# Query and value loads of a fused attention and feed-forward kernel move from ScalarE's DMA queue to SyncE's

## The chip, the cores and the metric

The kernel runs on one core of one Trainium2 chip. The metric is the device time of one execution in microseconds, the median of several timed runs. A further execution was taken with the hardware profiler; its rows are those shown here. An engine's own instructions run on the engine; the DMAs that it issues go through its sequencer, in the order of its queue, and the transfers themselves run beside all engines.

## The reference

Attention over 4 batches, 8 heads, 576 positions and 64 dimensions, in which each query keeps its 32 largest scores; then two feed-forward layers of 512 to 2048 to 512, the first with a rational function between its two products, the second with `h * cos(h)`:

```
scores = scale * np.matmul(q, k.transpose(0, 1, 3, 2))
kth = np.partition(scores, -top_k, axis=-1)[..., -top_k:-top_k + 1]
scores = np.where(scores >= kth, scores, -1000000000.0)
scores = scores - np.max(scores, axis=-1, keepdims=True)
attn = np.exp(scores)
attn = attn / (np.sum(attn, axis=-1, keepdims=True) + 1e-09)
x = np.matmul(attn, v)                       # then (batch * seq, 512)
h = x @ w_in                                 # first layer
P = a[0] + a[1] * h + a[2] * h**2 + a[3] * h**3
Q = 1.0 + np.abs(b[0]) * np.abs(h) + np.abs(b[1]) * h**2
x = (P / (Q + 1e-06)) @ w_out
h = x @ w_in2                                # second layer
out = (h * np.cos(h)) @ w_out2
```

## The kernel before

The 2304 tokens are 9 blocks (`k`) of 256. Attention goes by units: 72 of them, each one tile of 128 queries and one pair of heads, eight units to a block. Units 0 to 63 take their queries from one batch; in units 64 to 71 a tile holds the last 64 queries of two batches, so each such unit takes two sets of keys and two of values.

One unit goes through `qk` (TensorE makes scores in PSUM, ScalarE copies them out to `sS`), `topk` (VectorE finds the 32 largest of each row with eight-way maxima and replacements in `e`, ScalarE takes the exponential, VectorE masks and sums) and `av` (TensorE transposes `e`, ScalarE copies the transposes out as `pt...`, TensorE multiplies them with the values `v` in L383 and L388, ScalarE copies the result out to `xs`). `norm` divides by the sums. Scores are made one unit ahead: `qk(i + 1)` stands before `topk(i)`.

Products are taken in float32 split into a high and a low part. Queries are split by `split_q`: ScalarE writes `qh`, GpSimd subtracts and writes `ql` (both from `qr`). In the first units (`n < 2`) the raw queries and keys go into the product unsplit (L296). Keys are split once and stored in DRAM (`kdr`, from `kraw`); later units load the split keys from there with `load_k`.

The weights are split in the same way at the start (`conv`, 64 pieces, with tiles `raw` and `cb`, stored with SyncE's DMAs at L230 to L266), and their low parts are later streamed from DRAM: `stream` at L419, four buffers (`NST`), one buffer freed by TensorE's matmuls on it. The streams are `lo` (from `w1lo` and `w2lo`), `w1ol` and `w2o`; they feed the products at L442, L499 and L554. The feed-forward work of a block runs beside the attention of later blocks.

The loads that the change touches:

- `load_q` issues one load for two units, 256 KB into `qr`, of which there is one buffer (`QRB = 1`). So a load waits until the queries before it have been read: by GpSimd's `ql` where they are split, by TensorE where they are raw. `attention` calls it in the second fifth of every even unit (`p == LQ`), two units ahead.
- `load_v` issues one load for two units (two loads for each of the units 64 to 71), 320 KB into `v`, of which there are two buffers (`VB = 2`), freed by the value matmuls. `attention` calls it in the first fifth of a unit.
- `load_k` issues the loads of split keys on ScalarE's queue, 44 of them.

What sets the order: `attention` yields five pieces a unit, and the feed-forward steps have due times in pieces. The text of the program gives priorities. The order of each engine's queue is laid when the program is built, by a planner that plays the program through with its own estimates of durations (`TileContext(nc, schedule_with_timeline_sim=True)`): an instruction is placed when what it waits for is done in that play. On the chip each queue then keeps that order. `A`, `V` and `G` are ScalarE, VectorE and GpSimd behind a wrapper (`Windowed`) that, up to piece `PA = 90` on ScalarE, keeps an instruction behind those of `WA = 12` pieces earlier on that engine, DMA issues included; `SP` is SyncE without such a wrapper. All engine instructions issued through the wrapper carry its line, L78.

Of the kernel before, what the change touches and what calls it, by code (L numbers as in the profile page):

```python
# [87 lines left out]
def body(tc, out, qt, kt, vt, ident_d, w1_d, w1o_d, a_d, b_d, w2_d, w2o_d):  # L88
    nc = tc.nc
    V, A, G = Windowed(tc, nc.vector, WIN, PM), Windowed(tc, nc.scalar, WA, PA), Windowed(tc, nc.gpsimd, WG, PG)  # L90
    PE, SP = nc.tensor, nc.sync

    with ExitStack() as ctx:
# [57 lines left out]
        def load_q(i):  # L151
            k, pr = units[i][0] // 2, units[i][1]
            raw = att.tile([P, 2, BT], F32, tag="qr", bufs=QRB, name=f"qr{i}")
            A.dma_start(out=raw, in_=qt[k, pr])
            qpair[i // 2] = (raw,)

        def split_q(i):
# [21 lines left out]
        def load_v(i):  # L179
            n, pr = units[i]  # L180
            if i % 2 and not mixed[i]:
                ins[i][0][1] = vlast[0]
                return
            for j, (b, _) in enumerate(qts[n]):
                v = kv.tile([P, VW], F32, tag="v", bufs=VB, name=f"v{i}_{b}")
                A.dma_start(out=v, in_=vt[b, pr])
                ins[i][j][1] = vlast[0] = v

        load_q(0)
        load_k(0)  # L190
        ident = cst.tile([P, P], F32)
# [445 lines left out]
        def attention():  # L637
            load_k(1)
            load_v(0)
            qk(0)  # L640
            prev = None
            nrm, fresh, held = [], [], []
            for i in range(nu + 1):
                if LQ == 0 and i % 2 == 0 and i + 2 < nu:
                    load_q(i + 2)
# [8 lines left out]
                for p in range(5):  # L654
                    if p == 0 and prev is not None:
                        next(prev)
                    next(t, None)
                    if p == 0:
                        if prev is not None:
                            next(prev)  # L660
                        next(t, None)
                        if prev is not None:
                            av(i - 1)
                            if i % 4 == 0:
                                nrm.append(norm((i - 1) // 8, (i - 1) // 4 % 2))
                                next(nrm[-1])
                                fresh.append(nrm[-1])
                        if 0 < i < nu:
                            load_v(i)
                    if p == LQ > 0 and i % 2 == 0 and i + 2 < nu:  # L670
                        load_q(i + 2)
                    if p == SQ and i % 2 == 0 and 8 <= i + 2 < nu:
                        split_q(i + 2)
                    if fresh and p == 1:
                        next(fresh.pop())
                    if len(nrm) == 2 and (p == 1 or p == 4):
                        next(nrm[0 if p == 1 else 1], None)
                        if p == 4:
                            nrm = []
                    yield  # L680
# [56 lines left out]
```

## Time and profile before

| | us |
|---|---|
| timed runs | 1435.71, 1440.75, 1442.73 |
| median | 1440.75 |
| profiled execution | 1434.87 |
| its span, from the first to the last instruction | 1433.1 |

| engine | busy us | share of the span |
|---|---|---|
| TensorE, matmuls (PE) | 1248.5 | 87% |
| VectorE (DVE) | 1247.9 | 87% |
| ScalarE (ACT) | 1080.7 | 75% |
| GpSimd (POOL) | 632.7 | 44% |

The mean granted clock of TensorE was 0.934 of full speed. Two DMA queues carry the data: SyncE's 261.99 MB, ScalarE's 51.39 MB.

The shares are averages over stages with different limits, so the busy times by stage are read beside them. In the rows, `out<-in` names what an instruction writes and reads; SPq and ACTq are the queues of SyncE and ScalarE, and their lines are DMA issues, which do not count as busy time of the engine. `[2.92 <-ACT qh L78]` behind an instruction says that its engine sat idle 2.92 us before it, and what ended that. In a table of waits, `DVE u <- ACT u: 27.1, 8, 5.9` says that VectorE's work on `u` waited for ScalarE's `u` 27.1 us in all, 8 times, at most 5.9 us.

### The profile page before, as it was taken

To read this page: it belongs to the slowest core of one execution; us is meant where nothing else is said; L and a number is where in the kernel's file an instruction comes from. 1 tells how busy PE (TensorE), PEld (TensorE's weight loads), DVE (VectorE), ACT (ScalarE), POOL (GpSimd) and SP (SyncE) were. 2 spreads that over 40 slices of the span, in tenths; PEclk is the share of its full clock that TensorE was granted. 3 is DMA by queue.
4 is the path that set the end of the run, shared out by engine and by line. 5 is a ranking of instruction groups with operands and counts; after the bars stand their busy time and mean duration, and the time that the engine had idled before them with its cause. 6 is when DMAs were issued, how large, how long until landed. Compare 5 with 4: busy or idle time off the path is not lost.

```text
span 1433.1 us, 24823 instructions
## 1 busy us (share of the span) xinstructions
PE 1248.5 (87%) x8944; PEld 1106.0 (77%) x8944; DVE 1247.9 (87%) x2477; ACT 1080.7 (75%) x1873; POOL 632.7 (44%) x439
## 2 busy tenths in 40 slices
PE   5676777667996999899989988998999999999997
PEld 2344565556985888799878978897998899988986
DVE  6999878899999999999999999999999999645633
ACT  6787788766875887688878786887887788866743
POOL 3657455544543544455555454553545454420000
PEclk9776798779999999999999999999999999999999
DMA  7986867773555656466675665565565777656686
GB/s 242 313 274 206 264 209 223 267 273 126 176 189 188 214 201 217 151 203 236 224 234 203 209 216 168 189 218 178 195 222 198 264 259 277 219 202 221 222 278 220
DMA packets 141547, 314.96 MB, mean 220 GB/s; under 512 B 12016, under 2 KB 28528, under 8 KB 141424
## 3 DMA queue, kind: packets, MB, share of 16 engines
q1 hardware_dynamic: 122832, 261.99, 54.4%
q10 hardware_dynamic: 18592, 51.39, 10.6%
q8 instruction: 70, 1.15, 0.3%
q14 instruction: 53, 0.43, 0.1%
HBM read 278.20 MB, written 35.13 MB: 219 GB/s over the span
## 4 chain that ended last, share of the span: by engine, by line
DVE 41%; PE 31%; ACT 11%; DMA 9%; issue 5%; POOL 2%; ACTq 0%; SPq 0%; DVEq 0%; POOLq 0%
DVE e L78 18%; DVE hd L78 10%; DVE u L78 6%; PE o L554 6%; PE h L440 4%; PE h L441 4%; PE h L442 4%; DVE cb L78 2%; DMA raw<-w 2%; DMA w2o<-w2o 2%; PE y L499 2%; PE y L497 2%; PE y L498 2%; ACT L78 2%; DVE q L78 2%
## 5 line engine op out<-in xcount | busy, mean ns | idle before, releaser
L78 DVE MAX8 hd<-e 128x8 f32<-128x288 f32 (+1 forms) x576 | 322.2, 594 | 0.0
L554 PE MATMUL o<-w2o,gg 128*128 128x512 f32 x864 | 228.7, 402 | 10.4 <-DMA w2o<-w2o 10.3
L78 DVE MATCH_REPLACE8 e<-hd,e 128x288 f32<-128x288 f32 (+1 forms) x432 | 230.6, 538 | 0.0
L554 PEld LDWEIGHTS o<-w2o,gg 128*128 128x128 f32 x864 | 155.7, 192 | 41.8 <-DMA w2o<-w2o 14.1
L78 DVE TENSOR_TENSOR e<-sS 128x576 f32<-128x576 f32 x144 | 164.4, 1178 | 26.9 <-ACT sS L78 13.6
L440 PE MATMUL h<-xh,w1hi 128*128 128x256 f32 x576 | 172.3, 299 | 13.4 <-ACT hs L78 6.4
L497 PE MATMUL y<-gg,w1o 128*128 128x256 f32 x576 | 168.0, 292 | 16.9 <-ACT gg L78 16.9
L440 PE MATMUL h<-x2h,w2hi 128*128 128x256 f32 x576 | 165.8, 288 | 12.3 <-ACT w L78 8.0
L498 PE MATMUL y<-gg,w1o 128*128 128x256 f32 x576 | 167.9, 292 | 6.6 <-POOL gg L78 6.5
L441 PE MATMUL h<-xl,w1hi 128*128 128x256 f32 x576 | 167.9, 292 | 2.3 <-DVE xl L78 2.3
L499 PE MATMUL y<-gg,w1ol 128*128 128x256 f32 x576 | 166.3, 289 | 3.5 <-DMA w1ol<-w1ol 3.4
L78 POOL TENSOR_TENSOR gg<-u,gg 128x512 fp32r<-128x512 f32 x64 | 94.4, 1474 | 169.4 <-ACT gg L78 145.9
L441 PE MATMUL h<-x2l,w2hi 128*128 128x256 f32 x576 | 165.0, 287 | 3.6 <-DVE x2l L78 3.6
L442 PE MATMUL h<-xh,lo 128*128 128x256 f32 x576 | 166.9, 290 | 0.0
L442 PE MATMUL h<-x2h,lo 128*128 128x256 f32 x576 | 164.7, 286 | 0.0
L78 POOL TENSOR_TENSOR u<-u,w 128x512 f32<-128x512 f32 x64 | 94.2, 1471 | 156.6 <-ACT u L78 156.4
L78 DVE SCALAR_TENSOR_TENSOR e<-sS,hd,e 128x576 f32<-128x576 f32 x144 | 140.8, 987 | 10.0 <-ACT e L78 9.7
L78 ACT ACTIVATE e<-sS,nb 128x576 f32<-128x576 f32 x144 | 109.1, 772 | 40.4 <-DVE hd L78 40.3
L78 POOL TENSOR_TENSOR cb<-cb,raw 128x512 int32<-128x512 int32 x64 | 93.7, 1466 | 97.9 <-DVE cb L78 80.5
L497 PEld LDWEIGHTS y<-gg,w1o 128*128 128x128 f32 x576 | 112.6, 195 | 22.3 <-ACT gg L78 20.2
L440 PEld LDWEIGHTS h<-xh,w1hi 128*128 128x128 f32 x576 | 114.0, 198 | 18.6 <-ACT hs L78 8.5
L78 POOL TENSOR_TENSOR rr<-rr,hs 128x512 f32<-128x512 f32 x56 | 79.3, 1436 | 104.0 <-ACT rr L78 103.9
(1166 smaller groups left out, 3720.1 us busy)
## 6 DMA issues: line engine op xcount, KB each, us to landing
w2o<-w2o SPq DMA_DIRECT2D x144, 512.0 KB, 4.2
lo<-w1lo SPq DMA_DIRECT2D x72, 512.0 KB, 4.1
w1ol<-w1ol SPq DMA_DIRECT2D x72, 512.0 KB, 4.1
lo<-w2lo SPq DMA_DIRECT2D x72, 512.0 KB, 4.4
k<-kdr ACTq DMA_DIRECT2D x44, 576.0 KB, 5.1
raw<-w SPq DMA_DIRECT2D x32, 512.0 KB, 5.2
v<-vt ACTq DMA_DIRECT2D x48, 320.0 KB, 4.4
qr<-qt ACTq DMA_DIRECT2D x36, 256.0 KB, 4.2
```

The lines of the kernel that those rows point to most:

```text
L78: r = f(*a, **k)
L440: PE.matmul(h[:, i, :], wh, xh[:, c, :], start=(c == 0), stop=False)
L441: PE.matmul(h[:, i, :], wh, xl[:, c, :], start=False, stop=False)
L442: PE.matmul(h[:, i, :], lo[:, i, c, :], xh[:, c, :], start=False, stop=(c == NCC - 1))
L497: PE.matmul(y[:, c, :], w1o[:, f, cs], gh[:, i, :], start=(f == 0 and c % 2 == 0), stop=False, skip_group_check=True)
L498: PE.matmul(y[:, c, :], w1o[:, f, cs], gl[:, i, :], start=False, stop=False, skip_group_check=True)
L499: PE.matmul(y[:, c, :], wl[:, i, cs], gh[:, i, :], start=False, stop=(f == NF - 1), skip_group_check=True)
L554: PE.matmul(o[:, t, :], l[:, i, ts], wt[i][:, r], start=(f == 0 and r == 0 and l is gh), stop=(f == NF - 1 and l is gl), skip_group_check= ...
```

## The change

The loads of queries and of values are issued by SyncE instead of ScalarE. Tiles, buffers, bytes and the places of the calls stay as they are.

```diff
         def load_q(i):
             k, pr = units[i][0] // 2, units[i][1]
             raw = att.tile([P, 2, BT], F32, tag="qr", bufs=QRB, name=f"qr{i}")
-            A.dma_start(out=raw, in_=qt[k, pr])
+            SP.dma_start(out=raw, in_=qt[k, pr])
             qpair[i // 2] = (raw,)
...
             for j, (b, _) in enumerate(qts[n]):
                 v = kv.tile([P, VW], F32, tag="v", bufs=VB, name=f"v{i}_{b}")
-                A.dma_start(out=v, in_=vt[b, pr])
+                SP.dma_start(out=v, in_=vt[b, pr])
                 ins[i][j][1] = vlast[0] = v
```

## Rows read from the trace of the kernel before

**Rows 1.** The page: busy us, share of the span and instructions of each engine.

```profile
PE 1248.5 (87%) x8944; PEld 1106.0 (77%) x8944; DVE 1247.9 (87%) x2477; ACT 1080.7 (75%) x1873; POOL 632.7 (44%) x439
```

**Rows 2.** Busy us by stage: stretch, length, engines, TensorE's clock, DMA share, GB/s.

```profile
0.00:360.00 360.00, 250.17 (x1287) 183.97 (x1288) 317.65 (x636) 267.62 (x501) 185.30 (x134) 0.80 0.73 240
360.00:1240.00 880.00, 820.07 (x6416) 759.53 (x6415) 842.92 (x1706) 698.85 (x1208) 431.10 (x293) 0.97 0.62 210
1240.00:1433.10 193.10, 178.31 (x1247) 162.48 (x1246) 87.36 (x136) 114.24 (x165) 16.28 (x13) 1.00 0.68 227
```

**Rows 3.** The page's chain that ended last, shares by engine.

```profile
DVE 41%; PE 31%; ACT 11%; DMA 9%; issue 5%; POOL 2%; ACTq 0%; SPq 0%; DVEq 0%; POOLq 0%
```

**Rows 4.** VectorE's waits: who waited for whom, us in total, times, longest.

```profile
DVE u L78 <- ACT u L78: 27.1, 8, 5.9
DVE cb L78 <- ACT cb L78: 20.9, 11, 3.9
```

**Rows 5.** Query and value issues: ns least, median, most; first and last start.

```profile
L78 ACTq DMA_DIRECT2D qr<-qt x36: 334/335/445, 0.7 to 1154.0; - x36
...
L78 ACTq DMA_DIRECT2D v<-vt x48: 334/335/550, 1.2 to 1240.7; - x48
```

**Rows 6.** ScalarE in order of time at a value load: start, length, instruction.

```profile
524.79 0.20 ACT L78 ACTIVATE nb<-hd 128x2 f32<-128x2 f32 x1 [1.32 <-DVE hd L78]
524.80 0.33 ACTq L78 DMA_DIRECT2D v<-vt  x1
524.90 0.62 ACT L78 ACTIVATE r<-w 128x512 f32<-128x512 f32 x1
```

**Rows 7.** GpSimd's subtraction, the load behind it, tile ql and its waiters.

```profile
717.38 1.73 POOL L78 TENSOR_TENSOR ql<-qr,qh 128x512 fp32r<-128x512 f32 x1 [2.92 <-ACT qh L78]
...
719.14 0.34 ACTq L78 DMA_DIRECT2D qr<-qt  x1
...
L78 POOL TENSOR_TENSOR ql<-qr,qh x32: 1268/1440/2185, 120.0 to 1187.9; 128x512 fp32r<-128x512 f32 x32
...
  ACT q L78: 0.6, 1
  ACT r L78: 0.6, 1
```

**Rows 8.** SyncE's largest waits: from 0 to 360, then from 360 to 1240.

```profile
SPq L230 <- POOL cb L78: 62.4, 42, 3.7
...
SPq L419 <- PE h L442: 381.1, 92, 11.5
```

**Rows 9.** SyncE's queue in order of time around 719 us.

```profile
718.41 0.32 SPq L419 DMA_DIRECT2D w2o<-w2o  x1
721.63 0.37 SPq L419 DMA_DIRECT2D lo<-w1lo  x1
```

**Rows 10.** Loads and first readers, by time (L383: first to last start).

```profile
110.33 0.35 ACTq L78 DMA_DIRECT2D qr<-qt  x1
...
115.47 0.62 ACT L78 ACTIVATE qh<-qr 128x512 fp32r<-128x512 f32 x1
...
488.39 0.34 ACTq L78 DMA_DIRECT2D v<-vt  x1
...
L383 PE MATMUL sx<-pt28t,v x2: 272/273/274, 541.6 to 541.7; 128*128 128x128 f32 x2
...
747.16 0.61 ACT L78 ACTIVATE qh<-qr 128x512 fp32r<-128x512 f32 x1
```

**Rows 11.** Tile w2o: its readers' idle time that its loads ended, times.

```profile
  DMA w2o<-w2o: 24.4, 23
```

**Rows 12.** Value matmuls of units 44, 52 and 60, as in rows 10.

```profile
L383 PE MATMUL sx<-pt44t,v x2: 273/274/274, 807.1 to 807.2; 128*128 128x128 f32 x2
...
L383 PE MATMUL sx<-pt52t,v x2: 272/274/275, 947.0 to 947.1; 128*128 128x128 f32 x2
...
L383 PE MATMUL sx<-pt60t,v x2: 272/273/274, 1078.7 to 1078.8; 128*128 128x128 f32 x2
```

## The prediction

> **What bounds the kernel now.** I read the page first, then a table of busy time by stage, then the chain, then the waits. On the page no engine is the bound by its average: TensorE and VectorE are busy 87% of the span each, ScalarE 75%, GpSimd 44% [rows 1]. So the table by stage comes next [rows 2]. In the first 360 us, where weights are split while attention already runs, VectorE is busy 317.65 us and TensorE runs at 0.80 of its clock. From 360 to 1240 us, where attention and both feed-forward passes overlap, VectorE is busy 842.92 of 880 us (96%) and TensorE 820.07 (93%). In the last 193 us attention is over, and TensorE has 178.31 us. VectorE sets the pace until 1240 us, TensorE after that. The chain agrees: VectorE 41%, TensorE 31%, ScalarE 11%, DMA 9% [rows 3]. ScalarE counts only where the others wait for it; VectorE's two largest such waits are 27.1 and 20.9 us [rows 4].
>
> **The change part by part.** It takes 84 DMA issues from ScalarE's queue, 36 of queries and 48 of values, and puts them into SyncE's [rows 5].
>
> *What ScalarE gets back.* One issue takes 0.335 us at the median, so 84 x 0.335 = 28.1 us of its queue. Does its arithmetic stand still meanwhile? At 524.80 us a value load is issued, 0.01 us after `nb` began; `nb` takes 0.20 us, and the next instruction starts at 524.90, before `nb` has ended [rows 6]. The issue lies beside the arithmetic and costs nothing there. What is left is a queue that waits. A query load waits until GpSimd has read the old queries: the subtraction `ql` begins at 717.38, takes 1.73 us and so ends at 719.11, and the load goes out at 719.14 [rows 7]. What ScalarE loses by this stands among those who waited for `ql`: `q` 0.6 us and `r` 0.6 us [rows 7]. The visible gain is 1.2 us of idle ScalarE, by its share of the chain 1.2 x 0.11 = 0.1 us. The upper bound takes all of the queue time at that share, 28.1 x 0.11 = 3.1 us. I take 0.1, since the rows show the overlap itself.
>
> *What SyncE gets.* The same 28.1 us, in a queue that mostly waits: in the 880 us of the middle its stream loads (L419) wait 381.1 us for TensorE in one group alone [rows 8]. There is room, and what counts is order. Stream loads are released by TensorE's matmuls, value loads by its value matmuls, and one engine in order releases both, so neither holds the other for long. A query load is released by GpSimd, so it can hold SyncE's queue; behind it stand loads of weights, and behind those TensorE. In the sample, SyncE's neighbours went out at 718.41 and 721.63, and the query load at 719.14 falls between them [rows 7, 9]: at that place the price is nothing. Laid one place earlier, it would push the load of 718.41 to about 719.45, 1.0 us late.
>
> The Trainium skill ("DMA: Bandwidth & Descriptors", "Anatomy of one DMA") says that DMA engines do not wait on semaphores; the issuing sequencer does, ahead of dispatch. The trace agrees: the query load went out 0.03 us after `ql` ended [rows 7]. By that rule a query load holds whatever stands behind it in SyncE's queue, and the sum would be the first rival's.
>
> *What hides a late load.* The values issued at 488.39 are first read at 541.6, 53 us later; the queries issued at 719.14 are split at 747.16, 28 us later [rows 7, 10]. Some microseconds more in SyncE's queue don't show there. Cover is thin in the first stage: queries issued at 110.33 are split at 115.47, 5.1 us from issue [rows 10]. I take zero, and keep that stage as a rival.
>
> *What stays.* Bytes, arithmetic and buffers are the same, and the loads of split keys stay on ScalarE.
>
> *Sum.* Minus 0.1 us, with bounds of minus 3.1 and, from the first rival, plus 57, on a profiled execution of 1434.87 us, of which 1433.1 are span: about 1435. The median of the three timed runs is 1440.75, 5.9 us higher; they spread from 1435.71 to 1442.73. The comparison is with the median, so the forecast is 1441 us, no change that can be measured. About 0.5% (7 us) is what a measurement of this kernel can tell from no change.
>
> **The rivals.**
>
> *Slower: the query load holds the weight stream.* Place: SyncE's queue, 360 to 1240 us. It decides where the load is laid ahead of a stream load whose buffer is free before `ql` has ended. Price at most: one `ql` (1.44 us at the median) and one issue (0.33) for each of the 32 splits [rows 7], 32 x 1.77 = 57 us. For it: readers of `w2o` sat idle 23 times for a load already (weight loads and matmuls counted apart), 24.4 us in all [rows 11], so that stream has loads without slack; and GpSimd sat idle 2.92 us for ScalarE before `ql` began [rows 7], so its end can come late. Against it: most loads of that stream have slack, and the sample has room on both sides. I take a quarter of the 57 us, 14: 1455 us. Chance 0.15.
>
> *Faster: ScalarE answers sooner.* VectorE's two largest waits for ScalarE are 48 us together [rows 4]. With 84 entries fewer ahead of what VectorE waits for, a quarter of that might close: 12 us, 1429 us. For it: ScalarE is on the chain with 11% [rows 3]. Against it: the overlap [rows 6]. Chance 0.12.
>
> *Either way: the queues are laid anew.* A queue's order is not that of the program text. The planner lays it when the program is built, by due order and its own estimates of durations; with 84 entries in another queue it may lay others differently, on every engine. What an order is worth can be read from repeated work: eight units of attention with one block of feed-forward. Their first value matmuls start at 541.6 (unit 28), 807.1 (unit 44), 947.0 (unit 52) and 1078.7 (unit 60) [rows 10, 12]. That is 265.5 us for two blocks, then 139.9, then 131.7: a mean of 134.3 us with a spread (standard deviation) of 3.8. Nine blocks laid anew and independently give 3.8 x 3 = 11 us around no change. Chance 0.35, of which 0.095 falls below minus 7 us, 0.16 within and 0.095 above plus 7.
>
> *Slower: early queries come late.* In the first 360 us SyncE's largest wait is for GpSimd, 62.4 us in 42 pieces of up to 3.7 us [rows 8]; a query load behind such pieces eats up the 5.1 us from issue to use. If five loads come 2 us late each, it is 10 us: 1451 us. Against it: scores are made one unit ahead of VectorE's use, so a late query needn't stop it. Chance 0.05.
>
> That the change does nothing would need the loads to stay where they are; they go to another queue, so I give that no chance.
>
> **How the numbers follow.** No change by the sum has 0.33. Within 0.5%: 0.33 + 0.16 = 0.49, say 0.48. Faster: 0.12 + 0.095 = 0.215, say 0.22. Slower: 0.15 + 0.05 + 0.095 = 0.295, say 0.30. The likeliest case is no change: 1441 us, with 1434 to 1448 as its own range. The whole range is 1425 to 1461. Its low end takes in the faster case and one spread and a half of newly laid queues (16 us below), its high end the slower cases at their taken price and almost two spreads (20 us above). What lies beyond is the slower case near its bound of 57 us and the tails, about one tenth.
>
> **What the profile after would show.** If I am right: 84 issues under SyncE with the same 0.33 us and none of these under ScalarE; busy VectorE and TensorE from 360 to 1240 us within a few microseconds of before; idle time for `w2o` still near 24 us. First rival: SyncE's waits for `ql` reach tens of microseconds, and TensorE's waits for stream loads grow by ten or more. Second: VectorE's waits for ScalarE shrink by ten or more. Third: the blocks' lengths change while nobody waits for a moved load, and unrelated instructions stand in another order. Fourth: waits for `qr` or `v` in the first 360 us. The forecast is wrong if the time moves by over 7 us; by which of these, the waits tell.

## The result and the profile after

The changed kernel is slower: the ratio to the kernel before is 1.0134, with an interval of 1.0102 to 1.0166; the medians of four executions each are 1456.34 us after and 1441.74 us before, 14.6 us apart (1.0101; the recorded ratio is not formed from these two medians, and it is the ratios that are compared below). The forecast was no change (1441 us). The time lies inside the range given, the direction was missed.

One caution for reading the rows: the profiled execution of the changed kernel took 1466.88 us (span 1465.1), the longest of its four (the others 1458.57, 1454.12 and 1453.96), while the one of before (1434.87) lay below its median. So the rows below show 32 us where the medians show 14.6; what they tell is where the time went, more than how much.

The page after, busy time of the engines and the chain that ended last, to be held against [rows 1] and [rows 3]:

```profile
span 1465.1 us, 24836 instructions
PE 1263.3 (86%) x8944; PEld 1111.6 (76%) x8944; DVE 1257.4 (86%) x2477; ACT 1078.0 (74%) x1873; POOL 623.3 (43%) x439
DVE 38%; PE 31%; DMA 13%; ACT 11%; issue 5%; POOL 2%; SPq 1%; ACTq 0%; DVEq 0%; POOLq 0%
```

Each engine runs as many instructions as before. ScalarE, the engine that was relieved, is as busy as it was (1078.0 against 1080.7 us) and holds the same 11% of the chain. VectorE is 9.5 us busier, with the same 2477 instructions.

Busy time by stage after, columns as in [rows 2]; attention now ends near 1275 us instead of 1240:

```profile
0.00:360.00 360.00, 253.28 (x1318) 184.32 (x1319) 317.78 (x634) 267.77 (x503) 183.15 (x135) 0.81 0.74 241
360.00:1275.00 915.00, 833.50 (x6414) 766.85 (x6414) 852.19 (x1708) 696.93 (x1209) 424.36 (x293) 0.96 0.61 202
1275.00:1465.00 190.00, 176.57 (x1217) 160.40 (x1215) 87.39 (x136) 113.27 (x163) 15.77 (x12) 0.99 0.70 229
```

The first and the last stage are what they were. The middle one does the same work (1708 instructions of VectorE against 1706) in 915 us instead of 880. The granted clock of TensorE there, 0.96, is close to the 0.97 of before; a kernel that follows below (the old queue in the new order) is as late with 0.97, so the clock isn't where the time went. The first value matmuls of units 28, 44, 52 and 60 tell the same (behind the durations stand the first and the last start, as in [rows 10] and [rows 12]):

```profile
L383 PE MATMUL sx<-pt28t,v x2: 273/274/275, 556.0 to 556.2; 128*128 128x128 f32 x2
...
L383 PE MATMUL sx<-pt44t,v x2: 271/273/275, 828.3 to 828.4; 128*128 128x128 f32 x2
...
L383 PE MATMUL sx<-pt52t,v x2: 273/274/274, 965.9 to 966.0; 128*128 128x128 f32 x2
...
L383 PE MATMUL sx<-pt60t,v x2: 272/274/275, 1104.8 to 1104.9; 128*128 128x128 f32 x2
```

Against before that is 14.4, 21.2, 18.9 and 26.1 us late: no single stall, but a loss that grows, and once shrinks, over the whole middle.

The moved loads, and what SyncE's queue waits for after (columns as in [rows 5] and [rows 8], the waits over the whole span):

```profile
L154 SPq DMA_DIRECT2D qr<-qt x36: 328/346/541, 0.7 to 1183.8; - x36
...
L186 SPq DMA_DIRECT2D v<-vt x48: 327/346/975, 3.1 to 1273.2; - x48
...
SPq L419 <- PE h L442: 405.4, 120, 11.0
...
SPq L186 <- PE sx L388: 53.9, 33, 5.0
...
SPq L154 <- POOL ql L78: 49.5, 25, 5.2
```

The change does what it says: 84 issues under SyncE, 0.346 us each. SyncE's queue now waits 49.5 us for `ql` and 53.9 us for the value matmuls. But behind those waits hardly anyone waits longer than before. The readers of the streams `lo` and `w1ol` sat idle for their loads 12.0 us instead of 8.7, and 13.2 in the kernel below that has the moved loads back on ScalarE. The readers of `w2o` did so no longer than before (24.4 us in [rows 11]):

```profile
  DMA w2o<-w2o: 22.3, 24
```

So where is the time? VectorE sets the pace until attention ends, so its account is the one to draw up. Before, it was busy 1160.57 of 1240 us and idle 79.4; after, 1169.97 of 1275 and idle 105.0. The 35 us are 9.4 of longer work and 25.6 of idling. Some 3 us of these 35 come of where the stages are cut: VectorE's last work before 1240 us ended at 1239.3, the same instruction after ended at 1271.3, 32 us later, which is the difference of the spans. The idling by what ended it, over the whole span, first some groups of before, then those of after (columns as in [rows 4]; the wait for ScalarE's `u`, 27.1 us before, lies behind the end of attention in both and isn't part of this account):

```profile
DVE e L78 <- ACT sS L78: 13.6, 6, 6.6
DVE e L78 <- ACT e L78: 9.7, 14, 2.2
DVE u L78 <- POOL u L78: 8.1, 8, 2.5
```

```profile
DVE u L78 <- ACT u L78: 26.1, 8, 5.0
DVE e L78 <- ACT e L78: 25.6, 19, 3.8
DVE cb L78 <- ACT cb L78: 23.2, 8, 4.3
...
DVE e L78 <- ACT sS L78: 15.9, 9, 5.3
DVE u L78 <- POOL u L78: 13.6, 10, 2.6
...
DVE e L78 <- PE pp20t L377: 6.3, 1, 6.3
```

The largest term is the wait for ScalarE's exponential, 9.7 to 25.6 us; then GpSimd's `u` with 5.5 more, `cb` and `sS` with 2.3 each (smaller groups shrank). The single wait for a transpose of 6.3 us (`pp20t`) stands out, but all waits for transposes together grew by only 1.5 (13.4 to 14.9). None of these is a load of queries or values, and none is an engine that got more to do. The instructions stand in another order. The two built programs, listed by the names of their instructions without those that only wait, differ in 3912 lines on TensorE (each program has 8160 matmuls there; an instruction that moved counts as two lines), in 1424 on ScalarE and 202 on SyncE (84 of each are the moved loads), and in 824 on VectorE.

The longest of those waits for the exponential can be followed back. Three engines in order of time, after:

```profile
1157.03 0.58 PE L299 MATMUL sx<-k,qh 128*128 128x288 f32 x1 [4.20 <-DMA k<-kdr]
...
1159.09 2.76 PE L554 MATMUL o<-w2o,gg 128*128 128x512 f32 x6
1161.64 0.89 PE L370 MATMUL pp64a<-ident,e 128*128 128x128 f32 x4
```

```profile
1162.57 0.60 ACT L78 ACTIVATE pt64a<-pp64a 128x512 f32<-128x512 f32 x1 [2.60 <-PE pp64a L370]
...
1163.75 0.65 ACT L78 ACTIVATE sS<-sx 128x576 f32<-128x576 f32 x1 [0.58 <-PE sx L301]
...
1164.30 1.44 ACT L78 ACTIVATE e<-sS,nb 128x576 f32<-128x576 f32 x2
```

```profile
1159.85 1.41 DVE L78 MAX8 hd<-e 128x8 f32<-128x576 f32 x2
1165.10 0.82 DVE L78 SCALAR_TENSOR_TENSOR e<-sS,hd,e 128x576 f32<-128x576 f32 x1 [3.85 <-ACT e L78]
```

VectorE's maxima, the last that it does to `e` ahead of the exponential, ended at 1161.26. But on ScalarE the exponential stands behind the copy `pt64a`, which waits for TensorE, and on TensorE the transposes stand behind six feed-forward matmuls and those behind scores that waited 4.20 us for split keys. Each queue keeps its order, so a delay on TensorE reaches VectorE through work that has nothing to do with it.

This wait shows how a delay travels along the queues, but it is not a price of the order itself. In the kernel below that has the same order on all engines, and the loads on ScalarE, the same instruction waited 0.19 us:

```profile
1158.10 0.82 DVE L78 SCALAR_TENSOR_TENSOR e<-sS,hd,e 128x576 f32<-128x576 f32 x1 [0.19 <-ACT e L78]
```

What began it after, a load of split keys issued at 1146.77 that TensorE still waited for at 1157, is one of 44, and the slowest of them took 9.6 us to land (at most 7.7 in the kernel before). A moved query load (1149.86) and a moved value load (1150.62) went out while it was under way; whether they slowed it is not shown.

### The profile page after: what moved, and what is told of

It is laid out like the page before. It is cut to its first block, busy times and chain, and to the rows that moved or that the text cites. A ratio compares the mean times of both kernels' runs of the same rounds, so it can differ in the third digit from the quotient of the medians.

```text
span 1465.1 us, 24836 instructions
## 1 busy us (share of the span) xinstructions
PE 1263.3 (86%) x8944; PEld 1111.6 (76%) x8944; DVE 1257.4 (86%) x2477; ACT 1078.0 (74%) x1873; POOL 623.3 (43%) x439
## 4 chain that ended last, share of the span: by engine, by line
DVE 38%; PE 31%; DMA 13%; ACT 11%; issue 5%; POOL 2%; SPq 1%; ACTq 0%; DVEq 0%; POOLq 0%
DVE e L78 17%; DVE hd L78 9%; PE o L554 7%; DVE u L78 6%; PE h L440 4%; PE h L441 4%; PE h L442 4%; DMA w2o<-w2o 2%; DVE cb L78 2%; PE y L499 2%; PE y L497 2%; DMA raw<-w 2%; PE y L498 2%; DMA kdr<-kraw 2%; DVE q L78 2%
## 5 line engine op out<-in xcount | busy, mean ns | idle before, releaser
L554 PE MATMUL o<-w2o,gg 128*128 128x512 f32 x864 | 235.5, 408 | 9.6 <-DMA w2o<-w2o 9.4
L78 DVE TENSOR_TENSOR e<-sS 128x576 f32<-128x576 f32 x144 | 173.5, 1241 | 31.1 <-ACT sS L78 15.9
L78 POOL TENSOR_TENSOR gg<-u,gg 128x512 fp32r<-128x512 f32 x64 | 92.2, 1440 | 185.4 <-ACT gg L78 174.0
L78 POOL TENSOR_TENSOR u<-u,w 128x512 f32<-128x512 f32 x64 | 88.8, 1388 | 179.9 <-ACT u L78 156.0
L78 DVE SCALAR_TENSOR_TENSOR e<-sS,hd,e 128x576 f32<-128x576 f32 x144 | 141.6, 991 | 26.1 <-ACT e L78 25.6
L440 PEld LDWEIGHTS h<-x2h,w2hi 128*128 128x128 f32 x576 | 111.7, 194 | 16.5 <-ACT w L78 12.2
L497 PEld LDWEIGHTS y<-gg,w1o 128*128 128x128 f32 x576 | 114.1, 198 | 12.7 <-ACT gg L78 10.3
```

The costliest lines, as they stand in the source:

```text
L78: r = f(*a, **k)
L440: PE.matmul(h[:, i, :], wh, xh[:, c, :], start=(c == 0), stop=False)
L497: PE.matmul(y[:, c, :], w1o[:, f, cs], gh[:, i, :], start=(f == 0 and c % 2 == 0), stop=False, skip_group_check=True)
L554: PE.matmul(o[:, t, :], l[:, i, ts], wt[i][:, r], start=(f == 0 and r == 0 and l is gh), stop=(f == NF - 1 and l is gl), skip_group_check= ...
```

## The experiments

Two theories were to be told apart. One: SyncE's queue is at fault, where loads that wait for `ql` hold the stream (the prediction's first rival). Two: the new order of all queues is at fault, whatever queue the loads are in (its third rival). What tells them apart is a program whose order is given instead of planned: `ORDER` lists the instructions of a program as it was built before, and each engine's are chained in that sequence, without a wait between them (the code is shown in part). A moved load stands at the place that the planner gave it in time.

```python
    for q in queues.values():
        q.sort(key=lambda x: place[x.name])
        for x, y in zip(q, q[1:]):
            tc.add_manual_dep(y, x.name, mybir.DependencyInfo(mybir.DependencyClass.NoSync, mybir.DependencyReason.DATA), reason="pin")
```

**The new queue in the old order.** The changed kernel, all engines in the order of before:

```diff
+ORDER = (
...
         body(tc, out, *aps)
+        pin(tc)
```

> The loads stand in SyncE's queue as in the changed kernel, but every engine keeps the order that it has in the kernel before (each queue chained by edges without a wait; the moved loads stand in SyncE's queue at the place that the planner gave them in time). Theory 'order' (the 14.6 us come from queues laid anew on other engines): within 5 us of before, about 1441 us. Theory 'hold' (a query load that waits for GpSimd's ql holds SyncE's weight stream): the loss stays, about 1455 us, with waits of SyncE for ql of some 50 us as in the changed kernel and more idle time of TensorE for stream loads.

Measured: 1439.16 us against 1440.0, ratio 1.0002 (0.9985 to 1.002). The loss is gone, with all 84 loads on SyncE; on TensorE and VectorE no instruction stands elsewhere than in the kernel before. SyncE's waits for `ql`, and the idling of the `w2o` readers, in this kernel:

```profile
SPq L154 <- POOL ql L78: 59.8, 25, 5.4
```

```profile
  DMA w2o<-w2o: 33.7, 36
```

Both are larger here than in the changed kernel (49.5 and 22.3). So neither is what made that one slow.

**The old queue in the new order.** The changed kernel's order on all engines, with the loads back on ScalarE (issued past the wrapper, which the change took them out of too):

```diff
-            SP.dma_start(out=raw, in_=qt[k, pr])
+            nc.scalar.dma_start(out=raw, in_=qt[k, pr])
...
-                SP.dma_start(out=v, in_=vt[b, pr])
+                nc.scalar.dma_start(out=v, in_=vt[b, pr])
...
+        pin(tc)
```

> The loads stand in ScalarE's queue as before, but every engine keeps the order that it has in the changed kernel. Theory 'order': the loss comes with the order, about 1456 us (1450 to 1462). Theory 'hold': SyncE's queue is free of the loads, so about 1441 us.

Measured: 1460.42 us, ratio 1.0155 (1.0127 to 1.0183). The loss is back without one load moved. Its profiled execution (1460.25) lies at its median, so its rows are the fairer ones for the order's price. From 360 to 1240 us VectorE gets through 1655 instructions where before it was 1706, at the granted clock of before (0.97):

```profile
360.00:1240.00 880.00, 796.37 (x6144) 731.87 (x6143) 826.88 (x1655) 674.48 (x1169) 409.82 (x283) 0.97 0.61 202
```

Two of VectorE's waits in it:

```profile
DVE e L78 <- ACT e L78: 20.4, 18, 2.7
...
DVE e L78 <- PE pp20t L377: 6.1, 1, 6.1
```

Next to each other, in us, from the rows of these four and of two kernels that follow further down:

| | before | new queue, old order | after | old queue, new order | TensorE's order kept | third order |
|---|---|---|---|---|---|---|
| VectorE busy | 1247.9 | 1248.2 | 1257.4 | 1258.2 | 1236.2 | 1249.8 |
| VectorE waits for the exponential | 9.7 | 11.3 | 25.6 | 20.4 | 16.7 | 18.6 |
| ScalarE waits for raw keys (`kraw`) | 4.3 | 10.2 | 17.6 | 17.8 | 5.8 | 7.5 |
| `w2o` readers idle for its loads | 24.4 | 33.7 | 22.3 | 24.7 | 28.6 | 17.7 |
| ratio | 1 | 1.0002 | 1.0134 | 1.0155 | 0.9995 | 0.9929 |

In the first four kernels the first two lines go by the order and not by the queue. The third goes by it in the main, but doubles with the queue alone (4.3 to 10.2). No line by itself ranks the kernels: the third order, the fastest, has 18.6 us of waits for the exponential, and the kernel with two small loads moved, further down, is slower than before with 8.8.

**One of the two loads alone**, in the planner's own order. Only the line of `load_q`, then only that of `load_v`:

```diff
-            A.dma_start(out=raw, in_=qt[k, pr])
+            SP.dma_start(out=raw, in_=qt[k, pr])
```

> Only the 36 query loads move to SyncE; values stay on ScalarE; queues laid anew by the planner. Theory 'hold': query loads alone wait for ql, so nearly all of the loss, 1452 to 1457 us. Theory 'order': a third order, its time not tied to the loads, anywhere from 1430 to 1460 us.

```diff
-                A.dma_start(out=v, in_=vt[b, pr])
+                SP.dma_start(out=v, in_=vt[b, pr])
```

> Only the 48 value loads move to SyncE; queries stay on ScalarE; queues laid anew by the planner. Theory 'hold': value loads are released by TensorE in order and hold nothing, so 1438 to 1445 us. Theory 'order': a fourth order, anywhere from 1430 to 1460 us.

Measured: 1431.28 us, ratio 0.9941 (0.992 to 0.9962) with the queries alone, and 1443.71 us, 1.0032 (1.001 to 1.0055) with the values alone. The queries are the loads that wait for `ql` (67.4 us in that kernel), and by the first theory they had to cost; that kernel is faster than before. The parts don't add up to the whole either: minus 0.6% and plus 0.3% against plus 1.3%.

**Both loads moved, in a third order**: the changed kernel, all engines in the order that the planner had laid with the queries alone on SyncE.

```diff
+ORDER = (
...
+        pin(tc)
```

> Both loads stand in SyncE's queue as in the changed kernel, but every engine keeps the order of e3_queries_only (where only the queries had moved), the fastest order so far at 1431 us. Theory 'order' (the queue costs nothing, the order everything): 1431 us, 1427 to 1436, and so faster than both kernels with the very queues of the changed one. If the values in SyncE's queue cost something in some orders: above 1436 us.

Measured: 1428.51 us against 1437.59, ratio 0.9929 (0.9902 to 0.9957). The very change that lost 1.3% gains 0.7% in another order. This version is faster than both kernels. Against the queries alone (0.9941), in the same order, it has the values on SyncE as well, and no loss by it.

**What the first rival costs where it acts.** The new queue in the old order, but 26 query loads, from the eleventh on, laid earlier in SyncE's queue: one place, then further. The expectations below speak of three places for the second kernel; in the queue that it ran with, each of the 26 stands two places earlier. Shown is the queue's order, not the list itself:

```diff
-    [stream load A] [stream load B] [stream load C] [query load]
+    [stream load A] [stream load B] [query load] [stream load C]
...
-    [stream load A] [stream load B] [stream load C] [query load]
+    [stream load A] [query load] [stream load B] [stream load C]
```

> As e6_early_query_loads, with the 26 query loads one place earlier instead of three. It looks for the point from which a held SyncE queue costs time. A hold costs only beyond the slack of the weight loads (TensorE's idle time for them was 33.7 us with no place moved and 124.6 with three): SyncE's waits for ql near 100 us, TensorE's idle time for w2o 40 to 70 us, 1441 to 1456 us. If the price grew evenly with places, 1440 + 46 / 3 = 1455 us.

> As e1_new_queue_old_order, but each of the 26 query loads from the eleventh on is laid three places earlier in SyncE's queue, so ahead of three weight loads or stores that it stood behind. This makes the hold that my prediction feared on purpose. Theory 'a hold costs where it is laid early': SyncE stands some 5 us longer at each, 26 times, weight loads have a few us of slack, so 1450 to 1540 us, with TensorE's idle time for stream loads up from some 30 us to over 100. Theory 'a held SyncE queue is harmless wherever': 1440 us.

Measured: one place 1448.31 us, ratio 1.0058 (1.0035 to 1.0081); two places 1485.92 us, 1.0326 (1.0297 to 1.0354). SyncE's waits for `ql` and TensorE's for `w2o`, first with no, then one, then two places:

```profile
SPq L154 <- POOL ql L78: 59.8, 25, 5.4
PE o L554 <- DMA w2o<-w2o: 14.0, 16, 2.0
```

```profile
SPq L154 <- POOL ql L78: 114.9, 27, 8.7
PE o L554 <- DMA w2o<-w2o: 27.2, 22, 3.5
```

```profile
SPq L154 <- POOL ql L78: 191.0, 27, 14.4
PE o L554 <- DMA w2o<-w2o: 57.9, 27, 7.8
```

Here the mechanism shows both its signs. TensorE's waits grow by 13.2 and by 43.9 us, and the ratios, of some 1438 us, make 8 and 47 us. Per load that is 0.3 us for one place and 1.8 for two.

**Moves that should do nothing.** Two small loads of coefficients at the start go from SyncE to ScalarE, in the kernel before:

```diff
-        SP.dma_start(out=coef[:, 0:4], in_=a_d)
-        SP.dma_start(out=coef[:, 4:6], in_=b_d)
+        nc.scalar.dma_start(out=coef[:, 0:4], in_=a_d)
+        nc.scalar.dma_start(out=coef[:, 4:6], in_=b_d)
```

> The kernel before, with queries and values on ScalarE as they were; only the two loads of constants at the start (2 KB and 1 KB, used once) are issued by ScalarE instead of SyncE. The work of the queues is the same, but the planner lays all queues anew. Theory 'order': the time moves by an amount that has nothing to do with the two loads, anywhere from 1430 to 1460 us. If orders don't matter as such and the loss is due to where queries and values stand: 1437 to 1444 us.

And the loads of queries and values stay on ScalarE but go past the wrapper that ties them to the pieces:

```diff
-            A.dma_start(out=raw, in_=qt[k, pr])
+            nc.scalar.dma_start(out=raw, in_=qt[k, pr])
...
-                A.dma_start(out=v, in_=vt[b, pr])
+                nc.scalar.dma_start(out=v, in_=vt[b, pr])
```

> The kernel before; queries and values stay on ScalarE's queue, but are issued without the wrapper that keeps ScalarE's instructions within 12 pieces of each other at the start (the change takes the loads out of that wrapper too). Theory 'order': again all queues are laid anew, anywhere from 1430 to 1460 us. If leaving the wrapper is what costs: about 1456 us.

Measured: 1448.53 us, ratio 1.0065 (1.0044 to 1.0086), and 1447.48 us, 1.0076 (1.0047 to 1.0105). TensorE's order differs from before in 3440 and 3078 lines. Two loads of a few numbers per partition, used from 6.38 us on in the kernel before, cost 0.65%. Not by coming late themselves: VectorE's wait for them was 6.4 us before, and with them on ScalarE it is

```profile
DVE nega L78 <- DMA coef<-ma: 5.1, 1, 5.1
```

That it is the order that the planner then lays follows from the runs with a given order; for these two kernels it was not tested by itself.

**Which engine's order it is.** The changed kernel with one engine alone in the order of before, the others laid anew by the planner:

```diff
+ORDER = (
...
+        pin(tc)
```

> The changed kernel, with only TensorE's queue kept in the order of the kernel before; the planner lays the other queues around it. If what was lost came in with the order of TensorE's queue (VectorE waiting for transposes and ScalarE's copies behind it): 1436 to 1446 us. If it came with the orders of ScalarE's or VectorE's queues: 1450 us or more.

> The changed kernel, with only ScalarE's compute instructions kept in the order of the kernel before. If the loss came in with ScalarE's order: 1436 to 1446 us. If with TensorE's or VectorE's: 1450 us or more. Since the planner lays every queue around the kept one, both this and the one before may come out near 1441 us; then no single queue holds the loss.

> The changed kernel, with only VectorE's queue kept in the order of the kernel before. TensorE's and ScalarE's queues still differ much from before. If VectorE's order holds the loss: 1436 to 1446 us. If TensorE's or ScalarE's does: 1450 us or more.

Measured: with TensorE's order kept 1438.86 us, 0.9995 (0.9972 to 1.0018); with ScalarE's 1449.69 us, 1.0064 (1.0045 to 1.0084); with VectorE's 1457.32 us, 1.0124 (1.0095 to 1.0152). VectorE sets the pace, yet keeping its order gives nothing back that can be measured, and keeping TensorE's gives all. One reservation: an order that is kept on one engine draws the others after it. With TensorE's kept, VectorE's differs from before in 302 lines and ScalarE's in 540, where in the changed kernel it is 824 and 1424; with ScalarE's kept, TensorE's still differs in 786, with VectorE's kept in 2910. So TensorE's order is enough to get the time back; that nothing of the loss lies in the others' is not shown.

## Why the prediction was wrong, point by point

**ScalarE gets back next to nothing: right.** The sum had minus 0.1 us, at most minus 3.1. With everything else held in place the ratio is 1.0002 (0.9985 to 1.002), 0.3 us of 1440 with some 2.5 either way. The Trainium skill ("DMA: Bandwidth & Descriptors", "Issuing engines are not separate DMA queues") says that another issuing engine saves only its sequencer's time; the measurement agrees.

**SyncE has room, and what counts is the order in its queue: right.** At the planner's places the loads wait 49.5 us (changed kernel) to 72.5 us (VectorE's order kept) for `ql`. Where the queue can be told from the order, the time is not longer for it: 1.0002 against 1 in the old order, 1.0134 against 1.0155 in the new one. One place earlier each costs 0.3 us, where the step said that a stream load would go out 1.0 us late. Two places earlier each costs 1.8. That this is near the 1.77 taken as the most that one can cost is chance: SyncE's waits for `ql` grew there by 131.2 us, 5.0 for each of the 26 loads, with a longest of 14.4. One `ql` and one issue are no bound for what a load can hold, and the 57 us were none for the sum.

**Late loads are hidden: right.** In the changed kernel values are issued 39 to 71 us ahead of their first reader in units 4 to 62, queries 23 to 45 us from the seventh load on, and a load lands some 4 us after its issue (8.0 at most); the last eight units have the least, 10.3 us from issue. The readers of `qr` sat idle 4.4 us for a load, once, at the start of the kernel (before: 4.3, counted on weight loads and on matmuls), so the fourth rival didn't come.

**First rival: its first sign came, its second didn't.** Waits for `ql` of tens of microseconds were promised, and TensorE's waits for the stream to grow by ten. The first without the second is what the changed kernel shows. The mechanism is real, as the loads laid early show, but at the places that the planner gave the loads no price of it could be measured in the two orders in which the queue alone was changed.

**Second rival: absent.** VectorE's waits for ScalarE did not shrink; the exponential's grew by 15.9 us. Its price was also taken from the wrong places: of the 48 us, the 27.1 for `u` lie behind 1240 us, where the prediction itself has TensorE set the pace, and the 20.9 for `cb` in the first 360.

**Third rival: this is it, and its weighing is the step that failed.** It was written as something that the planner "may" do, at 0.35, beside "no change by the sum" at 0.33, as if the queues could also stay as they were. They can't: two small loads in another queue are enough for 3440 lines of difference on TensorE. The sum of direct costs was right at zero within some 2.5 us. What it left out, and so put at nothing, is the term for the new order, and that term by itself measured 1.0155 (1.0127 to 1.0183), the whole of the loss. The sum should not have had a case of its own: it gives the centre, and the third rival the spread around it. By that rival's own split, 0.095 to 0.16 to 0.095, the forecast would have been 0.27 faster, 0.46 no change and 0.27 slower. The number would have stood, and the chances would hardly differ; but the text would have named the order as what decides, and the result as one of its two likely sides.

Its size was nearly right, in part by luck: the 11 us rest on three block lengths of one order, one of them halved to count as two, and on blocks that vary independently. The five orders that the planner laid itself came to 0.9941, 1.0032, 1.0065, 1.0076 and 1.0134: a standard deviation of 0.0071, 10 us. Their mean is 1.0050, 7 us above no change, and four of the five are slower. That an order laid anew is on average worse than the one there was can't be settled by five, but the centre at no change was an assumption that no row of before supported.

**The signs.** "84 issues at 0.33 us": 0.346. "Busy VectorE and TensorE from 360 to 1240 us within a few microseconds": wrong, 821.75 and 798.50 us against 842.92 and 820.07, some 21 us less each, since the same work was spread over more time. "Idle time for `w2o` still near 24": 22.3. Of the third rival's signs all came: other block lengths (from unit 28 to 44 272.3 us instead of 265.5, then 137.6 and 138.9 instead of 139.9 and 131.7), nobody waiting for a moved load, unrelated instructions in another order.

**Open.** Which places in TensorE's order cost the time isn't found; the wait that was followed above is not one of them, since it is all but absent in the same order with the loads on ScalarE. That the rows make 32 us of what the medians show as 14.6 is partly the choice of the profiled executions; the rows of the old queue in the new order show the same terms at 1460.25 us.

## What to carry to other kernels

Where a planner lays the queues, every edit is two edits: what it does, and a new order for everything; here the second is worth minus 0.7% to plus 1.6% for the same work. Price the first from the profile, treat the second as certain and as a draw, and before judging an edit of this size hold the order fixed: the same change was 1.0134, 1.0002 or 0.9929 by the order alone. A load that waits in a shared queue cost nothing, 0.3 or 1.8 us here by its place, so look at what stands behind it, not at how long it waits.

## What the runs showed of the hardware

VectorE's busy time is no constant of the work: the same 2477 instructions took 1236.2 us (TensorE's order kept) to 1260.5 us (loads past the wrapper). GpSimd has a part in it. In the kernel before, VectorE's maximum and minimum of score halves (`e<-sS`) took 0.75 us at the median where GpSimd did no arithmetic beside it (45 of 144, none above 0.76) and 1.53 us where it did at some time meanwhile. In the changed kernel it is 0.75 (51 of 144) and 1.82, worked out from every such instruction and GpSimd's spans beside it (which are rough). The group's total rose from 164.4 to 173.5 us, nearly all of VectorE's 9.5, and it goes by the order: 164.3 us with the new queue in the old order, 173.9 with the old queue in the new one. One of each after, with GpSimd's instructions around them:

```profile
598.08 1.30 POOL L78 TENSOR_TENSOR ql<-qr,qh 128x512 fp32r<-128x512 f32 x1
...
624.02 1.73 POOL L78 TENSOR_TENSOR ql<-qr,qh 128x512 fp32r<-128x512 f32 x1
625.71 1.26 POOL L78 TENSOR_TENSOR gg<-u,gg 128x512 fp32r<-128x512 f32 x1
626.93 1.81 POOL L78 TENSOR_TENSOR gg<-rr,gg 128x512 fp32r<-128x512 f32 x1
```

```profile
600.58 0.73 DVE L78 TENSOR_TENSOR e<-sS 128x576 f32<-128x576 f32 x1
...
625.27 0.74 DVE L78 MAX8 hd<-e 128x8 f32<-128x576 f32 x1
625.94 1.65 DVE L78 TENSOR_TENSOR e<-sS 128x576 f32<-128x576 f32 x1
```

At 600.58 GpSimd has ended its work (599.38), and the instruction takes 0.73 us; at 625.94 it runs beside `gg` and takes 1.65. The maximum at 625.27, with one input, keeps its 0.74 us beside `ql`. The Trainium skill ("SBUF — State Buffer", "Who interferes with whom") says that a VectorE instruction with two inputs in SBUF contends with a GpSimd instruction that reads SBUF, and one with at most one such input does not, outside the 2-port modes, in which it uses both its pairs of ports; the trace agrees in these rows. So what an order costs is not only waiting: it also decides which instructions meet. It isn't the measure of an order either, since the fastest one is busy 1249.8 us on VectorE, more than before.
